# A sixth chunk with seven block products, w2's parts written over the weight sums, later key-value sums

## The chip, the cores and the metric

The kernel runs on one core of a Trainium2 chip. The core has TensorE (matrix products, with a separate weight load), VectorE, ScalarE and GpSimd, which work at the same time and wait for each other on semaphores, and SyncE, whose queue issues most of the loads and stores. In the profile they are PE (with PEld for the weight loads), DVE, ACT, POOL and SP. The metric is the time of one execution in microseconds; the times given are medians of several executions.

## The reference

One input x (2048 x 512) goes through two branches, and a gate mixes them.

```python
g = sigmoid((x * gate_w).sum(-1, keepdims=True))
# branch A: linear attention, 32 heads of 16 columns
q, k, v = heads(x @ wqkv)
phi(y) = concat([softmax(y @ w_phi), softmax(-(y @ w_phi))])
kv = sum over s of phi(k)[s]^T v[s];  z = sum over s of phi(k)[s]
a = (phi(q) kv / (phi(q) z + 1e-6)) @ wo
# branch B: 512 -> 1376 -> 512
b = mish(x @ w1 + b1) @ w2
out = g * a + (1 - g) * b
```

## The kernel before

**Two stages.** Stage A goes through the 2048 rows of x in eight chunks of 256, numbered 0 to 7 here as in the code, each of two tiles of 128 rows (t = 0, 1). It makes k, v and q of each tile. q is stored to memory (pqd); k gives the features E (differences from the largest and the smallest of each head, an exponential, sums, reciprocals, a scaling). From E and v come the key-value sums kvp, which stay in one PSUM buffer over all chunks, and E is added up into z. Stage B goes through four blocks of 512 rows: up product, Mish, down product, and for branch A the products with kv and wo.

**Split products.** Every operand is split into a high part (a rounded copy, made by ScalarE) and a low part (the remainder, made by VectorE or GpSimd). A product a w is high x high, high x low and low x high. One product of a tile (k0, k1, v0, v1, q0 or q1) is thus 12 matmuls with 512 columns.

**Chunks in FAST.** With x and the weights cut in two by rows and columns, four of the products (k and q of both tiles) can be made of seven block products (after Strassen and Winograd) of 6 matmuls each: 42 matmuls instead of 48. The seven products are s1 to s7. They need sums of blocks of x (`sa`, four additions on GpSimd; split into parts by `sh0`, `sh1` on ScalarE and `sl0`, `sl1` on GpSimd) and sums of blocks of the weights, made once: t1, t3, t2, t4, split by `h0` to `h3` and `l0` to `l3`. `bc` and `m7` are copies on ScalarE, `ca` and `qa` additions on VectorE. t1 to t3 lie in the tiles th and tl, which use the buffers w2a; t4 and the parts of the sums of x lie in sh and sl, which use the buffers w2b.

**Weights for stage B.** w1 and w2 are loaded in twelve pieces during stage A: `L0` to `L11` are loads (SyncE), `H` the high part (ScalarE), `O` the low part (GpSimd). Pieces 0 to 2 are w1a, 3 to 5 w1b, 6 to 8 w2a, 9 to 11 w2b; 5 and 11 have 512 columns, the others 1,024. The loads share two buffers, so a load waits for the `O` of the piece two before it. Pieces 6 to 11 write new tiles in the buffers w2a and w2b, and so wait until th, tl, sh and sl are no longer used.

**z.** The features of each chunk but the last two are added to two arrays in memory (zd) by an adding store from GpSimd's queue (`z0`, `z1`). In chunk 6 `zld` loads the first to the chip (zacc), `za` adds the second with an adding load through GpSimd's queue, and from there on `z0` and `z1` are additions on GpSimd.

**What sets the order.** Each engine runs its instructions in the order in which the code issues them. Strings of step names write that order out: FIRST for chunk 0, SECOND for 1, BEFORE for 2, SEVEN for each chunk in FAST, then THIRD, NEXT and LAST, and BLOCK strings for stage B. A name without a mark is a step of this chunk, ' of the chunk before, + of the block or part after, # a step on weights. Further steps: `xh`, `xl` split x of the next chunk, `ldx` loads x two chunks on, `mx mn d0 d1 E S rS ml` with the tile's number make the features, `ve` and `qe` copy v and q out of PSUM, `st` stores q, `kv` or `kk` makes the key-value sums (`kk` is the name where both chunks of a pair are taken in one place). `k`, `q` and some v products share three PSUM buffers in turn, so a product waits until the third last has been read out.

```python
FAST = range(3, 5)
at(key, f"ml{t}", lambda d=d: scale_by(d, V))
odd = c + 1 - c % 2
if odd + 1 in FAST:
    at(("A", odd + 1), "kk", kv)
else:
    at(key, "kv", kv)
```

Of the kernel before, what the change touches and what calls it, by code (L numbers as in the profile page):

```python
# [10 lines left out]
F32R = mybir.dt.float32r  # L11
# [4 lines left out]
P = 128  # L16
# [7 lines left out]
NCH = S // SC  # L24
# [7 lines left out]
GROW = FA % P  # L32
ORDER = [NFA - 1] + list(range(NFA - 1)) + list(range(NFA, NF))
WARM = 6
FAST = range(3, 5)

# [5 lines left out]
    S0 rS0 ml0 S1 rS1 ml1 q0 qe0 st0 q1 qe1 st1  # L42
"""
SECOND = """
    h0# h1# l0# h3# l1# l3# z0' z1' k0 xh mx0 mn0 d00 d10 xl ldx k1 E0 L0# L1# mx1 mn1 d01 d11 v0 E1 S0 rS0 ve0 ml0 t2# h2# z0
    v1 S1 rS1 ml1 ve1 q0 qe0 st0 q1 qe1 st1 l2# kv' kv
"""
BEFORE = """
    k0 z1' xh xl sa mx0 mn0 d00 d10 ldx k1 E0 H0# O0# L2# mx1 mn1 d01 d11 v0 E1 sh0 sl0 S0 rS0 ve0 ml0 z0
    v1 H1# O1# L3# S1 rS1 ml1 ve1 q0 qe0 st0 q1 sh1 sl1 qe1 st1  # L50
"""
SEVEN = """
    s1 bc s7 m7 kk s2 xh xl sa z1' mx0 mn0 s6 ca d00 d10 E0 ldx v0 ve0 sh0 sl0 more S0 rS0 s4 mx1 mn1 s5 qa st1 d01 d11 E1 ml0 z0
    v1 S1 rS1 s3 ve1 qe0 st0 ml1 sh1 sl1
"""
THIRD = """
    k0 z1' xh xl mx0 mn0 d00 d10 ldx k1 H6# E0 O6# L8# mx1 mn1 d01 d11 v0 H7# E1 O7# L9# S0 rS0 ml0 ve0 v1 H8# O8# L10# z0
    S1 rS1 ml1 ve1 q0 qe0 st0 q1 z1 qe1 st1 kv' kv
"""
NEXT = """  # L60
# [38 lines left out]
def tile_gated_mix(ctx: ExitStack, tc: tile.TileContext, xT, wv, wkT, wqT, bd, w1a, w1b, b1, w2a, w2b, wo, out):  # L99
# [23 lines left out]
    def k2(name, tag, dt=F32):  # L123
        return T([P, 512], dt, tag, {"pq": 3, "io": 4, "hl": 8}[tag], name)
# [81 lines left out]
    def at(key, name, fn):  # L206
        steps.setdefault((key, name), []).append(fn)
# [84 lines left out]
        pin(eng.tensor_mul(hv(d["E"][:, :]), hv(d["E"][:, :]), d["S"][:, :, None].to_broadcast([P, 2 * H, DH])))  # L292

    wkr, wqr = [T([P, NFB * 512], F32, "w1b", 2, n)[:, : KT * 512].rearrange("p (k f) -> p k f", f=512) for n in ("wkr", "wqr")]
    TT = [T([P, NFA * 512], F32R, "w2a", 2, n)[:, :].rearrange("p (i k f) -> p i k f", i=3, k=2) for n in ("th", "tl")]
    TS = [T([P, NFB * 512], F32R, "w2b", 2, n) for n in ("sh", "sl")]
    T4 = [t[:, :1024].rearrange("p (k f) -> p k f", k=2) for t in TS]
    SX = [t[:, 1024:2048].rearrange("p (i k f) -> p i k f", i=4, k=2) for t in TS]
    SR = []

    def tops():

        k0, k1, q0, q1 = raw = [x[:, i : i + 2, :] for x in (wkr, wqr) for i in (0, 2)]
        t1, t4, t3, t2 = raw
        hl = [(*(x[:, i, :, :] for i in range(3)), y) for x, y in zip(TT, T4)]
        at("W", "t1", lambda: pin(G_.tensor_sub(t1, k0, q0)))
# [82 lines left out]
    def a_ops(c):  # L389
        key = ("A", c)  # L390
        P_ = psA[c] = {}
        for t in range(2):
            d = {}
            Es[c, t] = d

            def k_(t=t):
                P_["k", t] = proj(xs[c], t, wkh, wkl, "a")

            def v_(t=t):
                P_["v", t] = proj(xs[c], t, wvh, wvl, "dn" if c or t else "kv")  # L400
# [24 lines left out]
            at(key, f"ve{t}", ve)  # L425
            if t and c in FAST:
                at(key, "qa", qa)
            else:
                at(key, f"qe{t}", qe)
            at(key, f"st{t}", st)  # L430
            feat_ops(key, t, lambda t=t: P_["k", t][:, :], d, t == 1 and c in FAST)
            at(key, f"ml{t}", lambda d=d: scale_by(d, V))

            def zs(t=t, d=d):
                if c >= NCH - 2:
                    end = c == NCH - 1
                    for sl in (slice(0, 512), slice(512, 1024)) if end and t else (slice(0, 1024),):
                        ins = pin(G_.tensor_add(Z["acc"][:, sl], Z["acc"][:, sl], d["E"][:, sl]))
                        if end and not sl.start:
                            tc.add_manual_dep(ins.ins, last[t].ins.name, SYNC, reason="VectorE's own sums first")  # L440
                elif c:
                    pin(G_.dma_start(zd[t][:, :], d["E"], accum_op=ALU.add))
                else:
                    pin(G_.dma_start(zd[t][:, :], d["E"]))

            at(key, f"z{t}", zs)
        if c == NCH - 2:
            def zld():
                Z["acc"] = k4("zacc", "z")
                pin(Sy.dma_start(Z["acc"], zd[0][:, :]))  # L450

            at(key, "zld", zld)
            at(key, "za", lambda: pin(G_.dma_start(Z["acc"], zd[1][:, :], accum_op=ALU.add)))

        def kv():
            if not kvs:
                kvs.append(psum("kvp", "kv")[:, : NG * 64].rearrange("p (g f) -> p g f", g=NG))
            (kvp,) = kvs
            for t in range(2):
                E, v = Es[c, t]["E"], vs[c, t]  # L460
                Ev = E[:, :].rearrange("p (a r b x) -> p b r a x", a=2, r=2, b=8)
                for u in range(8):
                    for r in range(2):
                        o = (u % 2) * 64 + 32 * r
                        mm(kvp[o : o + 32, u // 2, :], v[:, u * 64 + 32 * r : u * 64 + 32 * r + 32], Ev[:, u, r, :, :],
                           start=(c == 0 and t == 0 and u < 2), stop=(c == NCH - 1 and t == 1), skip_group_check=True)

        odd = c + 1 - c % 2
        if odd + 1 in FAST:
            at(("A", odd + 1), "kk", kv)  # L470
        else:
            at(key, "kv", kv)
        if c in FAST:
            fast_ops(c, key, P_)
# [395 lines left out]
    run(SECOND, ("A", 1), ("A", 0))  # L870
    run(BEFORE, ("A", 2), ("A", 1))
    for c in FAST:
        w = {3: "H2# O2# L4# H3# O3# L5#", 4: "H4# O4# L6# H5# O5# L7#"}[c]
        run(SEVEN.replace("more", w), ("A", c), ("A", c - 1))
    for c, text in ((NCH - 3, THIRD), (NCH - 2, NEXT), (NCH - 1, LAST)):
        run(text, ("A", c), ("A", c - 1), ("B", 0))
    for b in range(NB):
        run((BLOCK0, BLOCK1, BLOCK, BLOCK)[b], ("B", b), ("B", b - 1), ("B", b + 1))
# [61 lines left out]
```

## Time and profile before

| | |
|---|---|
| median of 3 runs | 457.06 us (456.77 to 458.35) |
| the profiled execution | 457.48 us |
| its span, first to last instruction | 455.6 us |
| TensorE's matmuls | 444.9 us busy, 2760 of them |
| VectorE | 318.3 us busy |
| ScalarE | 207.1 us busy |
| GpSimd | 153.7 us busy |
| mean granted clock of TensorE | 0.996 |

The page gives busy times by engine, a strip of forty slices, the queues, the chain of waits back from the last instruction, and groups of instructions. A row of a timeline has the start and the length in us, the engine, the line of the code, the operation, its tiles and shapes and a count; in square brackets stands how long the engine had been idle and what ended that. A row of TensorE's with x4 is four matmuls; since they overlap, the distance between two rows, not the length, is the pace. A row of waits has the total, the number and the longest. The row of a window has the stretch, its length, busy time and count of PE, PEld, DVE, ACT and POOL, the granted clock, the DMA share and GB/s. Rows of loads and stores give the count, KB and the median time from issue to landing.

### The profile page before, as it was taken

What the parts mean: (1) busy time and instruction counts of PE and PEld (TensorE: products, weight loads), DVE (VectorE), ACT (ScalarE), POOL (GpSimd) and SP (SyncE); (2) the same over time, 40 slices, a digit from 0 to 9 for tenths busy, and PEclk for the clock granted to TensorE, in tenths of its full rate; (3) what the DMA queues carried; (4) which work ended last, traced back from release to release, by engine and by line L of the source; (5) the groups of instructions that cost most, each with busy time, mean ns of one, the idle gap of its engine ahead of it and who ended that gap; (6) DMA issues with size and microseconds to landing.
All of it is one profiled execution on the core that took longest, in us unless ns stands there. A gap on an engine that the chain in (4) does not pass through costs nothing.

```text
span 455.6 us, 7013 instructions
## 1 busy us (share of the span) xinstructions
PE 444.9 (98%) x2760; PEld 363.6 (80%) x2760; DVE 318.3 (70%) x421; ACT 207.1 (45%) x286; POOL 153.7 (34%) x110
## 2 busy tenths in 40 slices
PE   7999699999999999999999999999999999999996
PEld 7888588888888888878787887887887888787885
DVE  2498887889597999979997985666967629611002
ACT  4772443726435564636347354434254553234220
POOL 2299465845724356320213212023212122221211
PEclk9999899999999999999999999999999999999999
DMA  7413845689596300222435050431141402030002
GB/s 281 160 62 122 201 125 139 149 204 264 163 322 149 116 24 1 72 68 71 138 101 154 17 148 21 109 114 54 24 117 56 112 19 92 1 81 13 1 0 94
DMA packets 27609, 47.41 MB, mean 104 GB/s; under 512 B 5940, under 2 KB 14132, under 8 KB 27576
## 3 DMA queue, kind: packets, MB, share of 16 engines
q1 hardware_dynamic: 25528, 39.88, 28.5%
q0 software_dynamic: 1904, 6.82, 7.8%
q8 instruction: 22, 0.36, 0.3%
q10 hardware_dynamic: 144, 0.26, 0.2%
q14 instruction: 11, 0.09, 0.1%
HBM read 23.87 MB, written 14.69 MB: 85 GB/s over the span
## 4 chain that ended last, share of the span: by engine, by line
PE 87%; DVE 0%; ACT 0%; issue 0%
PE up L111 27%; PE down L111 26%; PE proj L111 21%; PE wo L111 10%; PE num L111 2%; PE kvp L111 2%; DVE io L784 0%; ACT qs L131 0%; PE z L111 0%; ACT xh L131 0%; PE kvT L603 0%
## 5 line engine op out<-in xcount | busy, mean ns | idle before, releaser
L649 POOL TENSOR_TENSOR l<-act,h 128x512 fp32r<-128x512 f32 x44 | 61.4, 1397 | 219.1 <-ACT h L131 183.4
L131 ACT ACTIVATE act<-up,b1s 128x512 f32<-128x512 f32 x44 | 30.3, 688 | 88.6 <-PE up L111 88.5
L131 ACT ACTIVATE E<-E 128x1024 f32<-128x1024 f32 x32 | 33.6, 1060 | 55.6 <-DVE E L275 37.7
L292 DVE TENSOR_TENSOR E<-E,Sm 128x1024 f32<-128x1024 f32 x32 | 46.6, 1457 | 1.0
L281 DVE TENSOR_REDUCE Sm<-E 128x64 f32<-128x1024 f32 x32 | 38.7, 1211 | 4.9 <-ACT E L131 4.9
L111 PE MATMUL wo<-woh,ohl 128*128 128x512 f32 x128 | 40.8, 389 | 0.0
L111 PE MATMUL down<-w2ah,h 128*128 128x512 f32 x96 | 37.5, 390 | 0.0
L111 PE MATMUL down<-w2ah,l 128*128 128x512 f32 x96 | 37.4, 389 | 0.0
L111 PE MATMUL down<-w2al,h 128*128 128x512 f32 x96 | 37.3, 389 | 0.0
L784 DVE SCALAR_TENSOR_TENSOR io<-down,og_sb,io 128x512 f32<-128x512 f32 x16 | 11.1, 749 | 31.0 <-PE down L111 31.0
L111 PE MATMUL down<-w2bh,h 128*128 128x512 f32 x80 | 31.2, 390 | 0.0
L111 PE MATMUL down<-w2bl,h 128*128 128x512 f32 x80 | 31.1, 389 | 0.0
L111 PE MATMUL down<-w2bh,l 128*128 128x512 f32 x80 | 31.1, 389 | 0.0
L131 ACT ACT_TABLE_LOAD x20 | 25.7, 1283 | 10.4 <-PE up L111 10.1
L758 DVE TENSOR_TENSOR ohl<-num,ohl 128x512 fp32r<-128x512 f32 x16 | 10.2, 679 | 26.4 <-ACT ohl L131 26.4
L131 ACT ACTIVATE h<-act 128x512 fp32r<-128x512 f32 x44 | 27.8, 632 | 1.4
L111 PEld LDWEIGHTS wo<-woh,ohl 128*128 128x128 f32 x128 | 24.0, 188 | 5.1
L111 PE MATMUL up<-xbh,w1ah 128*128 128x512 f32 x96 | 26.2, 394 | 0.0
L111 PE MATMUL up<-xbh,w1al 128*128 128x512 f32 x96 | 25.7, 389 | 0.0
L111 PE MATMUL up<-xbl,w1ah 128*128 128x512 f32 x96 | 25.7, 389 | 0.0
L111 PE MATMUL wo<-wol,ohl 128*128 128x512 f32 x64 | 24.9, 389 | 0.0
L546 DVE TENSOR_TENSOR xbl<-xraw,xbh 128x1024 fp32r<-128x1024 f32 x8 | 10.0, 1288 | 19.8 <-ACT xbh L131 19.8
(156 smaller groups left out, 1006.0 us busy)
## 6 DMA issues: line engine op xcount, KB each, us to landing
xraw<-in_xT_dram SPq DMA_DIRECT2D x16, 512.0 KB, 5.4
eT<-tt SPq DMA_DIRECT2D x128, 64.0 KB, 2.0
zd<-E POOLq DMA_DIRECT2D x12, 512.0 KB, 6.6
pqd<-qs SPq DMA_DIRECT2D x16, 256.0 KB, 3.3
pq<-pqd SPq DMA_DIRECT2D x16, 256.0 KB, 2.9
out_dram<-io SPq DMA_DIRECT2D x16, 256.0 KB, 2.1
raw<-in_w1a_dram SPq DMA_DIRECT2D x3, 512.0 KB, 4.6
raw<-in_w2a_dram SPq DMA_DIRECT2D x3, 512.0 KB, 4.5
```

The costliest lines, as they stand in the source:

```text
L111: return pin(nc.tensor.matmul(*a, **k))
L131: return pin(A_.activation(out_, in_, fn, **k))
L281: pin(V.tensor_reduce(d["S"], hv(d["E"][:, :]), axis=AX.X, op=ALU.add))
L292: pin(eng.tensor_mul(hv(d["E"][:, :]), hv(d["E"][:, :]), d["S"][:, :, None].to_broadcast([P, 2 * H, DH])))
L546: last[h] = pin(V.tensor_sub(xb[b][1][:, :, sl], kt(raw[h], SC), f32(xb[b][0][:, :, sl])))
L649: pin(G_.tensor_sub(U[i]["l"], U[i]["a"], f32(U[i]["h"])))
L758: pin(V.tensor_sub(ohl[h, gp][:, 512:], num[h, gp], f32(ohl[h, gp][:, :512])))
L784: pin(V.scalar_tensor_tensor(io[t], dn[t], og_sb[:, i : i + 1], io[t], op0=ALU.mult, op1=ALU.add))
```

## The change

FAST takes chunk 5 in. Chunk 5 now runs by SEVEN; THIRD is gone. Pieces 6 to 11 of the weights are written into the tiles that hold the weight sums, part by part, so that a piece waits only for the readers of the columns that it overwrites. The additions of z on chip begin in chunk 5 instead of 6. The key-value sums of chunks 0 and 1 move into chunk 2, behind its k0, and those of 4 and 5 into chunk 6, behind its k0. h3, l1 and l3, h2 and l2 move from chunk 1 to chunk 2 or later in it, and two raw copies of the prologue come one weight split later. The pieces are now taken in the order 0 to 5, 11, 7, 8, 9, 6, 10.

```diff
-FAST = range(3, 5)
+FAST = range(3, 6)
...
 SECOND = """
-    h0# h1# l0# h3# l1# l3# z0' z1' k0 xh mx0 mn0 d00 d10 xl ldx k1 E0 L0# L1# mx1 mn1 d01 d11 v0 E1 S0 rS0 ve0 ml0 t2# h2# z0
-    v1 S1 rS1 ml1 ve1 q0 qe0 st0 q1 qe1 st1 l2# kv' kv
+    h0# h1# l0# z0' z1' k0 mx0 mn0 d00 d10 ldx k1 E0 L0# L1# xh mx1 mn1 d01 d11 v0 E1 S0 rS0 ve0 ml0 xl z0
+    v1 S1 rS1 ml1 ve1 q0 qe0 st0 q1 qe1 st1 t2#
...
+    s1 bc s7 m7 kk s2 xh xl zld sa z1' mx0 mn0 s6 ca d00 d10 E0 ldx v0 ve0 sh0 sl0 za more S0 rS0 s4 mx1 mn1 s5 qa st1 d01 d11 E1 ml0 z0
...
-    TT = [T([P, NFA * 512], F32R, "w2a", 2, n)[:, :].rearrange("p (i k f) -> p i k f", i=3, k=2) for n in ("th", "tl")]
-    TS = [T([P, NFB * 512], F32R, "w2b", 2, n) for n in ("sh", "sl")]
+    w2at = [T([P, NFA * 512], F32R, "w2a", 2, "w2a" + x) for x in "hl"]
+    TS = w2bt = [T([P, NFB * 512], F32R, "w2b", 2, "w2b" + x) for x in "hl"]
+    TT = [t[:, :].rearrange("p (i k f) -> p i k f", i=3, k=2) for t in w2at]
...
-                if c >= NCH - 2:
+                if c >= FAST[-1]:
...
-        if c == NCH - 2:
+        if c == FAST[-1]:
             def zld():
...
-        if odd + 1 in FAST:
+        if c <= FAST[-1]:
             at(("A", odd + 1), "kk", kv)
...
+    W["w2a"], W["w2b"] = (w2at, NFA * 512), (w2bt, NFB * 512)
...
-        w = {3: "H2# O2# L4# H3# O3# L5#", 4: "H4# O4# L6# H5# O5# L7#"}[c]
+        w = {3: "H2# O2# L4# H3# O3# L5#", 4: "H4# O4# L11# H5# O5# L7# H11# O11# L8#", 5: "H7# O7# L9# H8# O8# L6#"}[c]
         run(SEVEN.replace("more", w), ("A", c), ("A", c - 1))
-    for c, text in ((NCH - 3, THIRD), (NCH - 2, NEXT), (NCH - 1, LAST)):
+    for c, text in ((NCH - 2, NEXT), (NCH - 1, LAST)):
```

TensorE at the seam of chunks 1 and 2, before (E and v are features and values; the last two numbers of a row are the shape):

```order
L111 MATMUL proj_81_503<-wqh_15_122,xl_44_305 128x512 x2
L111 MATMUL kvp_83_520<-E_40_297,v_46_312 32x64 x16
L111 MATMUL kvp_83_520<-E_49_319,v_51_339 32x64 x16
L111 MATMUL kvp_83_520<-E_65_413,v_75_462 32x64 x16
L111 MATMUL kvp_83_520<-E_72_442,v_78_485 32x64 x16
L111 MATMUL proj_84_585<-wkh_11_118,xh_59_403 128x512 x2
```

and after:

```order
L107 MATMUL proj_81_498<-wqh_15_122,xl_44_305 128x512 x2
L107 MATMUL proj_87_524<-wkh_11_118,xh_66_427 128x512 x2
L107 MATMUL proj_87_524<-wkh_11_118,xh_67_428 128x512 x2
L107 MATMUL proj_87_524<-wkl_12_119,xh_66_427 128x512 x2
L107 MATMUL proj_87_524<-wkl_12_119,xh_67_428 128x512 x2
L107 MATMUL proj_87_524<-wkh_11_118,xl_68_429 128x512 x2
L107 MATMUL proj_87_524<-wkh_11_118,xl_69_430 128x512 x2
L107 MATMUL kvp_88_537<-E_40_297,v_46_312 32x64 x16
L107 MATMUL kvp_88_537<-E_49_319,v_51_339 32x64 x16
L107 MATMUL kvp_88_537<-E_61_404,v_75_457 32x64 x16
L107 MATMUL kvp_88_537<-E_72_437,v_78_480 32x64 x16
L107 MATMUL proj_92_612<-wkh_11_118,xh_66_427 128x512 x2
```

The twelve matmuls of chunk 2's k0 now stand ahead of the key-value sums.

ScalarE in chunk 4, from its first exponential to the copy of q (before):

```order
L131 ACTIVATE E_152_978<-E_152_978 128x1024
L131 ACTIVATE v_155_997<-proj_154_984 128x512
L131 ACTIVATE w1bh_129_805<-raw_128_803 128x1024
L131 ACTIVATE w1bh_129_805<-raw_131_809 128x512
L131 ACTIVATE E_162_1029<-E_162_1029 128x1024
L131 ACTIVATE v_165_1057<-proj_163_1035 128x512
L131 ACTIVATE qs_166_1059<-proj_143_877 128x512
```

and after, to the copies bc and m7 of chunk 5 (w2bh<-sraw are sh0 and sh1, w2bh<-raw is H11):

```order
L127 ACTIVATE E_153_983<-E_153_983 128x1024
L127 ACTIVATE v_156_1002<-proj_155_989 128x512
L127 ACTIVATE w2bh_21_130<-sraw_149_965 128x512
L127 ACTIVATE w1bh_129_805<-raw_128_803 128x1024
L127 ACTIVATE w1bh_129_805<-raw_131_809 128x512
L127 ACTIVATE w2bh_21_130<-raw_157_1008 128x512
L127 ACTIVATE E_164_1040<-E_164_1040 128x1024
L127 ACTIVATE v_167_1068<-proj_165_1046 128x512
L127 ACTIVATE qs_168_1070<-proj_143_877 128x512
L127 ACTIVATE w2bh_21_130<-sraw_149_965 128x512
L127 ACTIVATE proj_171_1084<-proj_169_1076 128x512
L127 ACTIVATE m7_172_1092<-proj_170_1077 128x512
```

H11 now stands between the two exponentials of chunk 4.

GpSimd from the stores of z of chunk 4 on, before (zd and zacc are the sums of z, w2al and w2bl the low parts of w2):

```order
L442 DMA zd0_124<-E_152_978 128x1024
L442 DMA zd1_125<-E_162_1029 128x1024
L513 TENSOR_TENSOR w2al_178_1108<-raw_156_1001,w2ah_177_1107 128x1024
L513 TENSOR_TENSOR w2al_178_1108<-raw_157_1005,w2ah_177_1107 128x1024
L513 TENSOR_TENSOR w2al_178_1108<-raw_179_1112,w2ah_177_1107 128x1024
L442 DMA zd0_124<-E_174_1089 128x1024
L442 DMA zd1_125<-E_182_1118 128x1024
L513 TENSOR_TENSOR w2bl_208_1314<-raw_184_1137,w2bh_207_1313 128x1024
L513 TENSOR_TENSOR w2bl_208_1314<-raw_188_1160,w2bh_207_1313 128x1024
L453 DMA zacc_205_1298<-zd1_125 128x1024
```

and after:

```order
L511 TENSOR_TENSOR w2bl_22_131<-raw_157_1008,w2bh_21_130 128x512
L439 DMA zd0_124<-E_153_983 128x1024
L335 TENSOR_TENSOR w2bl_22_131<-sraw_149_965,w2bh_21_130 128x512
L439 DMA zd1_125<-E_164_1040 128x1024
L450 DMA zacc_177_1108<-zd1_125 128x1024
L511 TENSOR_TENSOR w2al_20_129<-raw_158_1012,w2ah_19_128 128x1024
L511 TENSOR_TENSOR w2al_20_129<-raw_159_1016,w2ah_19_128 128x1024
L435 TENSOR_TENSOR zacc_177_1108<-zacc_177_1108,E_181_1123 128x1024
L435 TENSOR_TENSOR zacc_177_1108<-zacc_177_1108,E_191_1175 128x1024
L511 TENSOR_TENSOR w2bl_22_131<-raw_185_1147,w2bh_21_130 128x1024
```

The adding load of zacc (za) now comes before the low parts of pieces 7 and 8, and the two adding stores of chunk 5 have become additions behind them.

More of the change, by code (lines that the diff above doesn't have):

```diff
@@ L44 @@
 SECOND = """
-    h0# h1# l0# h3# l1# l3# z0' z1' k0 xh mx0 mn0 d00 d10 xl ldx k1 E0 L0# L1# mx1 mn1 d01 d11 v0 E1 S0 rS0 ve0 ml0 t2# h2# z0
-    v1 S1 rS1 ml1 ve1 q0 qe0 st0 q1 qe1 st1 l2# kv' kv
+    h0# h1# l0# z0' z1' k0 mx0 mn0 d00 d10 ldx k1 E0 L0# L1# xh mx1 mn1 d01 d11 v0 E1 S0 rS0 ve0 ml0 xl z0
+    v1 S1 rS1 ml1 ve1 q0 qe0 st0 q1 qe1 st1 t2#
 """
 BEFORE = """
-    k0 z1' xh xl sa mx0 mn0 d00 d10 ldx k1 E0 H0# O0# L2# mx1 mn1 d01 d11 v0 E1 sh0 sl0 S0 rS0 ve0 ml0 z0
+    z1' xh xl k0 kk h3# l1# l3# mx0 mn0 d00 d10 k1 E0 sa ldx h2# mx1 mn1 d01 d11 v0 E1 H0# O0# L2# l2# S0 rS0 ve0 ml0 sh0 sl0 z0
     v1 H1# O1# L3# S1 rS1 ml1 ve1 q0 qe0 st0 q1 sh1 sl1 qe1 st1
@@ L52 @@
 SEVEN = """
-    s1 bc s7 m7 kk s2 xh xl sa z1' mx0 mn0 s6 ca d00 d10 E0 ldx v0 ve0 sh0 sl0 more S0 rS0 s4 mx1 mn1 s5 qa st1 d01 d11 E1 ml0 z0
+    s1 bc s7 m7 kk s2 xh xl zld sa z1' mx0 mn0 s6 ca d00 d10 E0 ldx v0 ve0 sh0 sl0 za more S0 rS0 s4 mx1 mn1 s5 qa st1 d01 d11 E1 ml0 z0
     v1 S1 rS1 s3 ve1 qe0 st0 ml1 sh1 sl1
 """
[L56 to L59, printed above, removed]
 NEXT = """
-    lq0+ k0 xh xl mx0 mn0 d00 d10 ldx zld k1 H9# E0 O9# ldw0 L11# mx1 mn1 d01 d11 H10# E1 O10# ldw1 za S0 rS0 ml0 z0 v0 ve0 H11# O11#
+    lq0+ z1' k0 kk xh xl mx0 mn0 d00 d10 ldx k1 H9# E0 O9# ldw0 L10# mx1 mn1 d01 d11 H6# E1 O6# ldw1 S0 rS0 ml0 z0 v0 ve0 H10# O10#
     S1 rS1 ml1 z1 v1 ve1 q0 mx0+ mn0+ d00+ d10+ qe0 st0 q1 qe1 st1 E0+ lq1+
@@ L832, in tile_gated_mix @@
     fsplit(wkh, wkl, 2)
-    raw_k(0)
-    raw_k(1)
     k_part(0)
@@ L837, in tile_gated_mix @@
     fsplit(wkh, wkl, 3)
+    raw_k(0)
+    raw_k(1)
     k_part(1)
```

## The prediction

> **What bounds the kernel now.** I read the page's busy times first, then the waits of TensorE, then the chain of waits for the pace of a full stretch.
>
> ```profile
> PE 444.9 (98%) x2760; PEld 363.6 (80%) x2760; DVE 318.3 (70%) x421; ACT 207.1 (45%) x286; POOL 153.7 (34%) x110
> ...
> PE kvp L111 <- ACT xh L131: 3.5, 1, 3.5
> ...
> 40.00:60.00 20.00, 15.98 (x182) 12.93 (x182) 17.02 (x19) 6.01 (x9) 11.50 (x11) 0.91 0.58 141
> ...
> 166.53 2.72 PE down L111 x12
> ```
>
> TensorE is busy for 98% of the span. After the start it waits in one place only, ahead of the key-value sums (kvp) of chunk one; in that stretch, 40 to 60 us, it is busy for 15.98 us of 20 and its granted clock is 0.91. Everywhere else 12 matmuls of 512 columns take 2.72 us, so one costs 2.72 / 12 = 0.227 us. The time can fall by that one wait and by matmuls taken out, and it rises by every new wait of TensorE. The timeline of TensorE has the wait, and the same kind of work without it:
>
> ```profile
> 46.40 1.07 PE L111 MATMUL proj<-wqh,xl 128*128 128x512 f32 x4
> ...
> 53.17 1.08 PE L111 MATMUL kvp<-E,v 128*32 128x64 f32 x32 [3.46 <-ACT xh L131]
> 54.18 2.08 PE L111 MATMUL proj<-wkh,xh 128*128 128x512 f32 x4
> ...
> 58.01 1.08 PE L111 MATMUL proj<-wkh,xh 128*128 128x512 f32 x4
> ...
> 88.84 0.61 PE L111 MATMUL proj<-th,sl 128*128 128x512 f32 x2
> 89.39 1.99 PE L111 MATMUL kvp<-E,v 128*32 128x64 f32 x128
> ...
> 91.89 0.62 PE L111 MATMUL proj<-wkl,xh 128*128 128x512 f32 x2
> ```
>
> From 46.40 to 58.01 us (11.61 us) stand 16 matmuls of 512 columns and 128 of the sums. From 88.84 to 91.89 (3.05 us) stand 4 and 128, without a wait. Twelve more at 0.227 make 5.77 us. The wait, with the slow group behind it (2.08 us where 1.07 is usual), costs 11.61 - 5.77 = 5.84 us.
>
> **The change part by part.**
>
> *Sums later (chunk one).* TensorE goes from chunk one's last q product straight to k0 of chunk two; the sums follow. Are their inputs ready? The timelines of ScalarE and VectorE in chunk one:
>
> ```profile
> 37.86 1.06 ACT L131 ACTIVATE sh<-wkr 128x1024 fp32r<-128x1024 f32 x1 [4.19 <-POOL wkr L309]
> 38.83 1.14 ACT L131 ACTIVATE xh<-xraw 128x512 fp32r<-128x512 f32 x2
> 39.87 1.04 ACT L131 ACTIVATE E<-E 128x1024 f32<-128x1024 f32 x1
> ...
> 39.48 4.06 DVE L258 TENSOR_TENSOR xl<-xraw,xh 128x512 fp32r<-128x512 f32 x2 [1.51 <-ACT xh L131]
> ...
> 51.80 1.23 DVE L292 TENSOR_TENSOR E<-E,Sm 128x1024 f32<-128x1024 f32 x1
> ```
>
> Without sh and xh ahead of it the first exponential starts at 38.0 instead of 39.87. VectorE no longer spends 4.06 us on xl beside three operations of GpSimd; it does the differences of the second half first (to 40.4), then S0, rS0, ml0, xl, S1, rS1, ml1. Adding 1.2, 0.6, 1.2, 1.2, 1.2, 0.6, 1.2 from 40.4 ends ml1 at about 47.6, where it ended at 53.0. TensorE reaches k0 at 47.3 and the sums of the last tile at 47.3 + 2.7 + 1.5 = 51.5, so 4 us of slack: I take the whole 5.84 us as gone. The bounds are 0 (the wait stays) and 5.84. The two raw copies moved in the prologue, and the loads' new order, I cost at nothing: ScalarE stood idle before its next use there, and the pieces arrive several us before they are used, except where a term below says otherwise.
>
> *Seven products in chunk five.* Four products of 12 matmuls become seven of 6: 6 fewer, 6 x 0.227 = 1.36 us. It adds four sums and two remainders on GpSimd, four copies on ScalarE and one add on VectorE; chunks three and four carry the same load without a wait of TensorE.
>
> *Weight sums l1 and l3 move into chunk two.* They go to GpSimd beside ml0 and ml1 of chunk two. The rows that price this, from the timelines of VectorE and GpSimd, and the starts of chunks three and four with the first add of chunk three:
>
> ```profile
> 68.10 2.71 POOL L513 TENSOR_TENSOR w1al<-raw,w1ah 128x1024 fp32r<-128x1024 f32 x1
> 70.46 1.60 POOL L338 TENSOR_TENSOR sl<-sraw,sh 128x512 fp32r<-128x512 f32 x1
> ...
> 112.32 2.42 POOL L513 TENSOR_TENSOR w2al<-raw,w2ah 128x1024 fp32r<-128x1024 f32 x1 [1.90 <-ACT w2ah L131]
> ...
> 29.75 2.47 DVE L292 TENSOR_TENSOR E<-E,Sm 128x1024 f32<-128x1024 f32 x1
> ...
> 68.15 5.01 DVE L292 TENSOR_TENSOR E<-E,Sm 128x1024 f32<-128x1024 f32 x1
> ...
> 78.14 0.69 DVE L376 TENSOR_TENSOR proj<-proj,m 128x512 f32<-128x512 f32 x1
> ...
> 71.62 0.62 PE L111 MATMUL proj<-wkh,xh 128*128 128x512 f32 x2
> ...
> 86.58 0.62 PE L111 MATMUL proj<-wkh,xh 128*128 128x512 f32 x2
> ```
>
> Now GpSimd's remainder sl1 ends at 72.1, 0.4 us into chunk three; ml1 ends 1.1 us later. After the change chunk three begins at 71.62 - 5.84 = 65.8. An operation of GpSimd of 1,024 columns takes 2.42 us, so by estimate it does l1 from 48.2, l3 to 53.4, the sums sa to 56.9, O0 from 59.5 (ScalarE's cast ahead of it) to 62.0, sl0 to 63.3; ml0, held as in the rows, ends at 64.5 and releases its store; O1 and sl1 end near 69.9. If ml1 is again held until then it ends at 71.0; xl, two reductions and the add (1.3 + 1.2 + 0.7) end at 74.2. The product s4, which needs the add, comes 36 matmuls after the chunk's start, at 65.8 + 8.2 = 74.0. So 0.3 us late, between 0 (ml1 held as in the 2.47 us row) and 2. The Trainium skill, SBUF — State Buffer, "Who interferes with whom", says that whichever of the two engines issues first holds the shared port for one whole instruction, and the other then goes. The 2.47 us row agrees; the 5.01 us row does not, since it outlasts two instructions of GpSimd. By that rule this term would be zero and the sum 0.3 us lower.
>
> *H11 ahead of chunk four's second exponential.* This is the one new place where ScalarE waits for a load: piece 11 is loaded only once O4 has freed its buffer, and ScalarE's next work (the exponential, v's and q's evictions, the copy bc that TensorE's s6 of chunk five needs) stands behind it. I keep the profile's times from here on, leaving out the shift so far. Timelines of ScalarE, SyncE's queue and TensorE, and the page's landing times:
>
> ```profile
> 80.05 1.06 ACT L131 ACTIVATE E<-E 128x1024 f32<-128x1024 f32 x1 [3.83 <-DVE E L275]
> ...
> 96.33 1.06 ACT L131 ACTIVATE E<-E 128x1024 f32<-128x1024 f32 x1 [5.20 <-issue]
> ...
> 102.19 1.06 ACT L131 ACTIVATE E<-E 128x1024 f32<-128x1024 f32 x1 [2.85 <-DVE E L273]
> ...
> 139.17 0.63 ACT L131 ACTIVATE w2bh<-raw 128x512 fp32r<-128x512 f32 x1 [7.18 <-DMA raw<-in_w2b_dram]
> ...
> 85.90 3.74 SPq L169 DMA_DIRECT2D raw<-in_w1b_dram  x2
> ...
> 130.36 0.51 SPq L169 DMA_DIRECT2D raw<-in_w2b_dram  x1
> ...
> 103.68 1.07 PE L111 MATMUL proj<-wkh,xh 128*128 128x512 f32 x4
> ...
> raw<-in_w1b_dram SPq DMA_DIRECT2D x1, 256.0 KB, 2.8
> ```
>
> Chunk three has the same order up to there: its load L4 is issued 85.90 - 80.05 = 5.85 us after the first exponential, so L11 at 96.33 + 5.85 = 102.2. A quarter megabyte landed in 2.8 us once, and in 139.17 - 130.36 = 8.8 us once (this same piece, in a crowded stretch). I take 2.8, since the earlier loads are then nearly in: H11 at 105.0, the exponential at 105.5 instead of 102.19, bc done 3.1 us later, at 108.6. TensorE wants it at 103.68 plus 18 matmuls, 107.8: 0.8 us. VectorE, whose S1 waits for the exponential, has that, a sum, a reciprocal, a scaling, xl, two reductions and the add of chunk five to go through, 1.1 + 1.2 + 0.6 + 1.2 + 1.3 + 1.2 + 0.7 = 7.3 us, to 112.8, when TensorE, so delayed, wants it: together 1.1 us, with 8.8 us landing 7.1.
>
> *Sums of z on chip from chunk five.* zld now waits in SyncE's queue for chunk four's store of z0, and GpSimd's za waits for zld; O7, O8, the adds, O9 and L10 are queued behind za, H10 behind L10, and q0's eviction in chunk six behind H10. TensorE's k1 of chunk seven takes q0's PSUM buffer.
>
> ```profile
> zd<-E POOLq DMA_DIRECT2D x12, 512.0 KB, 6.6
> ...
> raw<-in_w2b_dram SPq DMA_DIRECT2D x2, 512.0 KB, 4.4
> ...
> zacc<-zd SPq DMA_DIRECT2D x1, 512.0 KB, 6.4
> zacc<-zd POOLq DMA_DIRECT2D x1, 512.0 KB, 6.6
> ...
> DMA to landing us min/median/max: 3.0/6.5/11.0
> ...
> 143.12 2.39 POOL L438 TENSOR_TENSOR zacc<-zacc,E 128x1024 f32<-128x1024 f32 x1 [5.84 <-DMA zacc<-zd]
> ...
> 88.85 1.51 DVE L292 TENSOR_TENSOR E<-E,Sm 128x1024 f32<-128x1024 f32 x1
> ```
>
> (The row of minimum, median and maximum is that of the twelve stores zd.) z0's store goes out at 106.9, after O11; +6.5 is 113.4; +6.4 is 119.8 for za; O7 then runs to 123.1 and O8 to 125.5. The load za lands at 126.4, two adds end at 131.2, O9 at 133.6, L10 lands at 138.0, and H10 with two evictions ends at 140.1. TensorE ends chunk five at 103.68 + 66 x 0.227 + 1.1 = 119.7, and k1 of chunk seven comes at 119.7 + 2.7 + 2.1 + 16.3 = 140.8, plus the next term: about 1 us of slack, no cost. But ml1 of chunk five now lies beside O7: in chunk three ml1 began 88.85 - 86.58 = 2.27 us after the chunk's end, so here at 122.0, and TensorE wants it at 119.7 + 2.7 + 1.5 = 124.0. Held as in the 2.47 us row, which also began inside an operation of GpSimd, it ends at 124.5: 0.5 us; as in the 5.01 us row 2.6; free, 0. I take 0.5.
>
> *Sum.* The profiled execution took 457.48 us (span 455.60 and 1.88 around it). 457.48 - 5.84 - 1.36 + 0.3 + 1.1 + 0.5 = 452.18. The median of the runs shown, 457.06, is 0.42 below that execution: 451.8 us.
>
> **The rivals.**
> - All new waits are hidden (ml1 slips in, L11 lands before H11): 457.48 - 7.20 - 0.42 = 449.9. For it: TensorE ran for 400 us without a wait. Against: H11's load cannot leave before O4.
> - Piece 11 lands late, as in the 8.8 us row: 7.1 instead of 1.1 us, and the clock falls once more as after the 3.46 us wait (1.0): 458.8, within 0.5% of before.
> - GpSimd is held by za. With both z transfers through GpSimd's queue at the largest landing, 11.0, and L10 at 8.8, H10's chain ends at 140.1 + 4.5 + 4.4 + 4.4 = 153.4; k1 waits 153.4 - 141.3 = 12.1, and 1.0 for the clock: 451.8 + 13.1 = 464.9, slower. It decides against the change from some 8 us of added landing on. For it: these rows lie in the same crowded stretch. Against: medians leave the slack.
> - The wait of chunk one only moves: if ml1 still ended at 53.0, TensorE would idle 1.5 us behind k0, so 453.3 at most; it stays faster.
>
> **How the numbers follow.** What a measurement of this kernel tells from no change is 0.5%, 2.3 us: faster is below 454.8, slower above 459.3. My own sum has 0.46 (450.7 to 454.5), all hidden 0.23, late piece 0.12 (half-late ones still faster), za 0.11, the moved wait 0.08. Faster: 0.46 + 0.23 + 0.08 = 0.77; same 0.12; slower 0.11. The range runs from 449.6, just under the case with all hidden, to 457.5, into the late piece; it leaves out za and the worst of the late piece.
>
> **What would show it.** Right: TensorE without a gap from 47 to 52 us and no group of 2.08 us; 2754 matmuls; small waits of TensorE on ScalarE near 102 us and on VectorE near 117 and 68. Wrong: a wait of TensorE above 3 us at chunk five's s6, at the sums in chunk six, or at k1 of chunk seven, with ScalarE waiting for a raw piece or GpSimd for zacc.

## The result, and the profile after

The changed kernel takes 460.3 us (median of 5 executions, 458.63 to 460.79), where the kernel before takes 457.06. The ratio is 1.0059, with a 95% interval of 1.004 to 1.0079. So it is slower by about 0.6%, and the prediction, 451.8 us and faster (449.6 to 457.5), was wrong in its sign and in its range. The profiled execution took 458.63 us, with a span of 456.7.

Chunks are counted from 0 here, as before. Some of the quoted expectations count them from 1; the text behind each names the place again.

The page of the changed kernel, busy times and the chain that ended last:

```profile
PE 443.1 (97%) x2754; PEld 361.0 (79%) x2754; DVE 332.9 (73%) x423; ACT 208.5 (46%) x289; POOL 164.2 (36%) x116
...
PE 65%; DVE 7%; issue 1%
```

and TensorE's waits after it (total, number, longest):

```profile
PE kvp L107 <- DVE E L288: 4.1, 1, 4.1
PE proj L107 <- ACT proj L127: 1.8, 1, 1.8
...
PE proj L107 <- DVE proj L373: 1.0, 1, 1.0
```

TensorE has its 2754 matmuls, six fewer, but VectorE is now 7% of the chain, and there is a wait of 4.1 us for VectorE that the kernel before did not have and the prediction did not name. TensorE's timeline after shows both ends of the story:

```profile
46.07 1.07 PE L107 MATMUL proj<-wkh,xh 128*128 128x512 f32 x4
...
48.88 1.99 PE L107 MATMUL kvp<-E,v 128*32 128x64 f32 x128
50.80 1.20 PE L107 MATMUL proj<-wkh,xh 128*128 128x512 f32 x4
...
103.08 0.73 PE L107 MATMUL proj<-wkh,xh 128*128 128x512 f32 x2 [1.78 <-ACT proj L127]
...
139.52 1.10 PE L107 MATMUL kvp<-E,v 128*32 128x64 f32 x64
...
156.36 1.08 PE L107 MATMUL kvp<-E,v 128*32 128x64 f32 x32 [4.05 <-DVE E L288]
157.37 2.08 PE L107 MATMUL up<-xbh,w1ah 128*128 128x512 f32 x4
```

The seam of chunks 1 and 2 has no gap any more (46.07 to 50.80). TensorE reaches the first sums of chunk 7 at 139.52, then waits 4.05 us for the last tile's scaled features, and stage B begins at 157.37. The same two rows before:

```profile
144.00 1.10 PE L111 MATMUL kvp<-E,v 128*32 128x64 f32 x64
...
157.16 1.20 PE L111 MATMUL up<-xbh,w1ah 128*128 128x512 f32 x4
```

TensorE had come 4.5 us earlier to chunk 7's sums, and all of it was given back within the rest of that chunk. The two windows of 20 us (length, then busy time and count of PE, PEld, DVE, ACT, POOL, then clock) say who was busy there, before:

```profile
120.00:140.00 20.00, 20.00 (x208) 16.75 (x208) 14.51 (x20) 6.97 (x10) 8.49 (x6) 1.00 0.93 250
```

and after:

```profile
120.00:140.00 20.00, 20.00 (x142) 16.33 (x134) 19.86 (x20) 7.14 (x9) 18.70 (x8) 1.00 0.69 230
```

VectorE has the same 20 instructions, in 19.86 instead of 14.51 us; GpSimd is busy for 18.70 us instead of 8.49. Both engines' timelines after, VectorE first:

```profile
118.02 1.51 DVE L288 TENSOR_TENSOR E<-E,Sm 128x1024 f32<-128x1024 f32 x1
119.45 5.69 DVE L254 TENSOR_TENSOR xl<-xraw,xh 128x512 fp32r<-128x512 f32 x2
...
137.95 1.69 DVE L269 TENSOR_TENSOR E<-pq,mx 128x512 f32<-128x512 f32 x1
139.56 2.89 DVE L271 TENSOR_TENSOR E<-mn,pq 128x512 f32<-128x512 f32 x1
...
154.36 1.85 DVE L288 TENSOR_TENSOR E<-E,Sm 128x1024 f32<-128x1024 f32 x1
```

```profile
115.10 0.88 POOL L450 DMA_DIRECT2D zacc<-zd  x1 [8.93 <-DMA zacc<-zd]
115.67 6.10 POOL L511 TENSOR_TENSOR w2al<-raw,w2ah 128x1024 fp32r<-128x1024 f32 x2
121.73 5.66 POOL L435 TENSOR_TENSOR zacc<-zacc,E 128x1024 f32<-128x1024 f32 x2
...
135.71 3.38 POOL L511 TENSOR_TENSOR w2bl<-raw,w2bh 128x1024 fp32r<-128x1024 f32 x1
139.06 2.85 POOL L435 TENSOR_TENSOR zacc<-zacc,E 128x1024 f32<-128x1024 f32 x1
```

GpSimd waits 8.93 us before it can issue za. Behind za stand O7, O8 and the two additions of z, and they come out without a pause, 115.67 to 127.4 us, with O9 and O6 right after them. Right there VectorE has to split x for chunk 7 (xl), and the pair takes 5.69 us. A second heap comes after a pause of 1.23 us, an addition, O10 and another addition, and meets the differences of q (pq), 1.69 and 2.89 us. The kernel before, VectorE:

```profile
121.35 1.29 DVE L258 TENSOR_TENSOR xl<-xraw,xh 128x512 fp32r<-128x512 f32 x2 [2.55 <-ACT xh L131]
125.07 0.69 DVE L266 TENSOR_REDUCE mx<-proj 128x32 f32<-128x512 f32 x1 [2.42 <-PE proj L111]
...
137.38 0.68 DVE L273 TENSOR_TENSOR E<-pq,mx 128x512 f32<-128x512 f32 x1
137.98 0.69 DVE L275 TENSOR_TENSOR E<-mn,pq 128x512 f32<-128x512 f32 x1
141.39 0.69 DVE L266 TENSOR_REDUCE mx<-proj 128x32 f32<-128x512 f32 x1 [2.72 <-PE proj L111]
...
154.37 1.91 DVE L292 TENSOR_TENSOR E<-E,Sm 128x1024 f32<-128x1024 f32 x1
```

The account of VectorE, from the start of xl to the end of the last scaling: before, 121.35 to 156.28 is 34.9 us, of which it waited 2.42 + 2.72 and three times 0.2 us, so its work takes about 29.1. After, 119.45 to 156.21 is 36.8 without a wait. That is 7.7 us more, nearly all in two places: 5.69 - 1.29 = 4.4 for xl and 1.69 + 2.89 - 1.37 = 3.2 for the differences. TensorE was ready for the result at 156.36 - 4.05 = 152.3. Undisturbed, and if it never had to wait for TensorE, VectorE would have been done at 119.45 + 29.1 = 148.6, 3.7 us ahead; 7.7 - 3.7 = 4.0 is the wait. (This is an account of one trace and comes out by construction; whether GpSimd's order is the cause, e1 and e6 test.)

### The profile page after: what moved, and what is told of

Read it like the earlier page. It is cut to its first block, busy times and chain, and to the rows that moved or that the text cites. A ratio compares the mean times of both kernels' runs of the same rounds, so it can differ in the third digit from the quotient of the medians.

```text
span 456.7 us, 7015 instructions
## 1 busy us (share of the span) xinstructions
PE 443.1 (97%) x2754; PEld 361.0 (79%) x2754; DVE 332.9 (73%) x423; ACT 208.5 (46%) x289; POOL 164.2 (36%) x116
## 4 chain that ended last, share of the span: by engine, by line
PE 65%; DVE 7%; issue 1%
PE up L107 27%; PE down L107 26%; PE wo L107 10%; PE num L107 2%; DVE E L288 1%; DVE E L271 1%; DVE Sm L277 1%; DVE E L269 1%; DVE mx L262 1%; DVE xl L254 1%; DVE Sm L285 0%; DVE io L782 0%; DVE mn L262 0%; PE kvp L107 0%; PE z L107 0%
## 5 line engine op out<-in xcount | busy, mean ns | idle before, releaser
L647 POOL TENSOR_TENSOR l<-act,h 128x512 fp32r<-128x512 f32 x44 | 60.2, 1370 | 220.5 <-ACT h L127 184.8
L288 DVE TENSOR_TENSOR E<-E,Sm 128x1024 f32<-128x1024 f32 x32 | 49.1, 1534 | 1.0
```

The costliest lines, as they stand in the source:

```text
L647: pin(G_.tensor_sub(U[i]["l"], U[i]["a"], f32(U[i]["h"])))
```

## The experiments

Theory P (the port): the work of GpSimd that piles up behind za comes out as one burst beside VectorE's two-operand work, and VectorE becomes what ends stage A. Rival L (piece 11): ScalarE's wait for the load of piece 11 is the main loss. Rival W (amount): GpSimd simply has too much to do with the sixth chunk run by SEVEN, wherever that work stands. The first expectations also name a load theory: VectorE itself has too much to do from chunk 5 on, whoever works beside it. The table has all runs. "Sums" is the time at which the key-value sums at the seam begin and "B" the time at which stage B begins, both in the profiled execution. From B to the end of the span it is 298.4 us, or up to 2 more where a long wait left TensorE's clock low, so what differs lies ahead of B.

| kernel | median us | ratio to before, interval | sums | B | between |
|---|---|---|---|---|---|
| changed | 460.3 | 1.0059 (1.004 to 1.0079) | 48.88 | 157.37 | 108.5 |
| e1_za_behind | 455.92 | 0.9982 (0.9949 to 1.0016) | 48.00 | 153.69 | 105.7 |
| e2_h11_behind | 459.66 | 1.008 (1.0034 to 1.0126) | 48.09 | 154.59 | 106.5 |
| e3_seam_alone | 452.86 | 0.9916 (0.9884 to 0.9948) | 48.30 | 151.27 | 103.0 |
| e4_six_alone | 465.39 | 1.0177 (1.013 to 1.0224) | - | 163.05 | - |
| e5_both_behind | 453.6 | 0.9927 (0.9894 to 0.9959) | 48.58 | 152.83 | 104.3 |
| e6_z_late | 459.18 | 1.0027 (0.9999 to 1.0055) | 49.07 | 154.84 | 105.8 |
| e7_seam_sums | 450.42 | 0.985 (0.9821 to 0.9878) | 50.19 | 151.40 | 101.2 |
| e8_z_late_h11 | 454.93 | 0.9947 (0.9927 to 0.9967) | 49.13 | 153.49 | 104.4 |
| e9_all_three | 452.4 | 0.9896 (0.9876 to 0.9917) | 48.55 | 152.00 | 103.5 |
| e7_again | 450.97 | 0.987 (0.9847 to 0.9893) | 49.31 | 150.52 | 101.2 |
| e3_again | 453.59 | 0.9944 (0.9911 to 0.9976) | 49.40 | 152.63 | 103.2 |
| after_again | 462.96 | 1.0133 (1.0065 to 1.0201) | 49.32 | 164.44 | 115.1 |

The kernel before had medians of 457.16, 457.71 and 457.36 us in the three groups of runs (first four, next four, last four of the table's experiments).

### e1: za behind the low parts

```diff
- ... ve0 sh0 sl0 za more S0 rS0 s4 ...
+ ... ve0 sh0 sl0 more za S0 rS0 s4 ...
```

> Changed kernel, with the adding load za behind O7 and O8 in GpSimd's queue instead of ahead of them. Port theory (GpSimd's work piles up behind za and comes out in one burst beside VectorE's xl of chunk seven, which takes 5.69 us instead of 1.29, and stage A ends with VectorE): xl takes 1.3 to 2.5 us, TensorE's wait of 4.05 us at chunk seven's sums falls below 1.5 and the slow group behind it goes: 455 to 456.5 us. Load theory (VectorE has too much to do from chunk five on, whoever is beside it): 460, the wait stays at 4 us. Piece-11 theory (ScalarE's wait for piece 11 makes VectorE late): 460, since that wait is not touched.

Measured: 455.92 us. VectorE's groups from 115 to 158 us:

```profile
L271 DVE TENSOR_TENSOR E<-mn,pq 128x512 f32<-128x512 f32 x2 | 3.6, 1784 | 0.0
L269 DVE TENSOR_TENSOR E<-pq,mx 128x512 f32<-128x512 f32 x2 | 2.4, 1188 | 0.0
L254 DVE TENSOR_TENSOR xl<-xraw,xh 128x512 fp32r<-128x512 f32 x2 | 1.3, 684 | 0.0
```

No instruction was taken out; one load went two places back in GpSimd's queue. xl is 1.3 us again, of TensorE's waits in stage A only those of 1.8 and 1.0 are left, and the median is 4.4 us lower. The differences of q are as long as before the edit, and without xl's 4.4 us VectorE just keeps ahead (7.7 - 4.4 = 3.3 is less than the 3.7 us). Both engines have the same instructions as in the changed kernel, so neither the load theory nor W can explain the 4.4 us. Theory P holds, in place and in size. From the seam's sums to B it is only 2.8 us less than in the changed kernel, although chunk 7 has lost its whole wait. In this execution TensorE ran slowly behind the wait of 1.8 us for piece 11 (granted clock 0.65 from 104 to 108 us). From the end of that wait to the sums of chunks 4 and 5 it needed 16.78 us, 1.6 more than in the changed kernel.

### e2: piece 11 behind the sums of x for chunk 5 (sh1, sl1)

```diff
- 4: "H4# O4# L11# H5# O5# L7# H11# O11# L8#"
+ 4: "H4# O4# L11# H5# O5# L7#"       and " H11# O11# L8#" at the end of chunk 4
```

> Changed kernel, with H11, O11 and L8 behind sh1 and sl1 of chunk four instead of ahead of its second exponential. Piece-11 theory: VectorE's wait of 3.06 us and TensorE's of 1.78 us go, and with them most of the loss: 455 us or less, wait at chunk seven's sums below 2 us. Port theory: the two waits go, but za and the burst behind it come earlier by the same 3 us, so xl still takes over 4 us and TensorE still waits some 3 to 4 us at chunk seven's sums: 457 to 459. Load theory: as the port theory, 457 to 458.

Measured: 459.66 us. The wait of 1.8 us on ScalarE is gone, but:

```profile
PE kvp L107 <- DVE E L288: 4.1, 1, 4.1
```

```profile
L254 DVE TENSOR_TENSOR xl<-xraw,xh 128x512 fp32r<-128x512 f32 x2 | 5.7, 2876 | 0.0
```

Stage B begins 2.8 us earlier than in the changed kernel, 0.8 of it because the seam does. The burst came along with its chunk and cost the same: the wait behind it is 4.06 us. Rival L is a second, smaller loss and not the main one. The median hardly moved (460.3 to 459.66) and lies just above the 457 to 459 that P expected; the executions spread widely, and the profiled one, 456.63 us, is the shortest.

### e3 and e4: each half alone

e3 is the kernel before with the new orders of chunks 1 and 2; e4 is the changed kernel with the old ones.

```diff
  e3, from the kernel before:
- SECOND, BEFORE, the two raw copies as before;   if odd + 1 in FAST:
+ SECOND, BEFORE, the two raw copies as changed;  if c < 2 or odd + 1 in FAST:
  e4, from the changed kernel:
- SECOND, BEFORE, the two raw copies as changed;  if c <= FAST[-1]:
+ SECOND, BEFORE, the two raw copies as before;   if 2 <= c <= FAST[-1]:
```

> Kernel before, with the order of chunks one and two and the prologue of the changed kernel alone (sums of chunks zero and one behind k0 of chunk two); chunk five, the pieces and the sums of z as before. Port theory: VectorE waited for TensorE before (2.4 and 2.7 us in chunks six and seven), so it can follow; the 5.84 us come through but for a wait for the piece loads: 451.5 to 454. Load theory: the end of stage A is VectorE's and does not move: 456 to 458, with a wait of TensorE of 4 us and more at chunk seven's sums. The wait at the seam itself is gone by both.

> Changed kernel with the order of chunks one and two and the prologue as before (the wait of TensorE at the seam of chunks one and two comes back, 5.84 us). Port and piece-11 theories: TensorE is late by 5.84 us, so VectorE's lateness in chunks six and seven falls into that: the wait at chunk seven's sums goes, 459 to 461.5, about the time of the changed kernel. If each part instead has its price by itself: 460.3 + 5.8 = 466.

Measured: 452.86 and 465.39 us, 4.3 less and 8.2 more than before. In e3 only one wait is left behind the start, 0.9 us at s4 of chunk 3. e4 has all the others:

```profile
PE kvp L107 <- DVE E L288: 4.6, 2, 4.1
PE kvp L107 <- ACT xh L127: 3.5, 1, 3.5
```

My expectation for e4 fell. I had thought that the 4.1 us wait exists only because TensorE arrives 4.5 us early, so that the old wait at the seam would swallow it. It does not: 8.2 - 4.3 = 3.9, near the 3.2 us that the whole change costs. za waits for transfers that start with chunk 4's store of z, so the burst has its place in the chunks, not in time: za goes out 11.85 us after TensorE's wait for piece 11 has ended, where it was 12.02 in the changed kernel. The wait at the end is there whether chunk 5 begins early or late. The two halves simply add.

### e5: both moved

e1's and e2's edits together.

> The load of the z sums stands behind the two low parts of chunk six on GpSimd's queue, and piece 11 of w2 stands behind the sums of chunk five, both together. If the port was the main loss and the wait for piece 11 a separate second one, the two add: 455.9 with the load behind, less the 1.8 us that the sums of chunk six still wait for the copy there, gives 453.5 to 454.8, and no wait of 1.8 us on ScalarE is left in the trace. If the two long differences of chunk eight (3.6 and 2.4 us in both runs so far) still keep VectorE as what ends stage A, taking the 1.8 us away gives nothing: 455.5 to 456.5.

Measured: 453.6 us, and no wait of 1.8 us on ScalarE. The two losses are separate and add. But two smaller waits have come up that the changed kernel hid behind the larger ones; TensorE's timeline:

```profile
118.93 0.65 PE L107 MATMUL kvp<-E,v 128*32 128x64 f32 x32 [0.98 <-DVE E L288]
...
136.68 1.21 PE L107 MATMUL proj<-wkh,xh 128*128 128x512 f32 x4 [0.55 <-ACT qs L127]
```

The first is the sums of chunks 4 and 5, late because ml0 of chunk 5 lies beside O8 (2.67 us instead of 1.2). The second is k1 of chunk 7, which waits for q's eviction behind H10.

### e6 and e8: z as before, without and with e2's edit

```diff
- SEVEN: xl zld sa ... sl0 za more ...      NEXT: ldx k1 ... ldw1 S0
+ SEVEN: xl sa ... sl0 more ...             NEXT: ldx zld k1 ... ldw1 za S0
- if c >= FAST[-1]:  (z added on chip)      if c == FAST[-1]:  (zld, za)
+ if c >= NCH - 2:                          if c == NCH - 2:
```

> The changed kernel, with the sums of z as in the kernel before: chunk six still adds by DMA, and the two loads of the z sums stand in chunk seven. GpSimd is then spared the two additions of chunk six (2.4 to 2.9 us each) and isn't held before the low parts 7 and 8. If the burst behind the held load is the cause, xl of chunk seven is 1.3 us again, the wait for the scaled sums there goes, and the time is 454.5 to 457, as with the load moved behind. If it is the amount of GpSimd's work in the sixth chunk with its seven products, the time stays at 459 to 460.5. If the load now holds the low parts of chunk seven instead and the burst comes one chunk later, beside the differences of chunk eight, it is 457 to 460 with the wait at chunk eight.

> The sums of z as before, and piece 11 behind the sums of chunk five, together. By the sum of the parts it is 1.0 to 1.8 us less than with the sums of z as before alone, and so 453 to 455.5 by the burst theory; if GpSimd's amount of work is the cause it is 457.5 to 459.

Measured: 459.18 and 454.93 us. In e6's profile xl and the differences are as short as in the kernel before:

```profile
L271 DVE TENSOR_TENSOR E<-mn,pq 128x512 f32<-128x512 f32 x2 | 1.4, 683 | 0.0
L269 DVE TENSOR_TENSOR E<-pq,mx 128x512 f32<-128x512 f32 x2 | 1.4, 680 | 0.0
L254 DVE TENSOR_TENSOR xl<-xraw,xh 128x512 fp32r<-128x512 f32 x2 | 1.3, 685 | 0.0
```

Of the wait at chunk 7's sums 0.58 us is left. The trace of e6 is what P expects (455.04 us in the profiled execution), its median what W expects. That execution is the fastest of ten; the others reach to 460.6, with granted clocks down to 0.991. e8, with the same work for GpSimd and without the wait of 1.9 us on piece 11, lies at 454.93 in P's range, which speaks against W. That e6's median is 4.3 us above e8's where 1.0 to 1.8 were expected is not settled: the wait for piece 11 and the clock behind it would do it, as e1's trace shows, but no trace of one of e6's longer executions was taken.

### e7 and e9: the weight sums left in chunk 1

```diff
- SECOND: h0# h1# l0# z0' z1' k0 ...               BEFORE: ... k0 kk h3# l1# l3# mx0 ...
+ SECOND: h0# h1# l0# h3# l1# l3# z0' z1' k0 ...   BEFORE: ... k0 kk mx0 ...
```

e7 is e3 with this edit, e9 is e5 with it.

> The orders of chunks two and three alone (452.9), with the three steps of the weight sums (the copy of one, two low parts on GpSimd) left in chunk two as before. In the orders alone they stand in chunk three, where GpSimd holds the port against xl (6.1 us for 1.3) and the product s4 waits 0.9 us for VectorE. If that is what the wait comes from, xl is 1.3 us, the wait goes, and the time is 451.5 to 452.3. If the low parts hold VectorE in chunk two instead, the wait moves there: 452.6 to 454.

> The changed kernel with three places mended at once: the load of the z sums behind the low parts 7 and 8, piece 11 behind the sums of chunk five, and the steps of the weight sums left in chunk two. With the first two the profile began stage B at 152.83 us; the 1.0 us wait of the fourth sum of chunk four should go as it did with the orders alone, so stage B begins near 151.9 and the time is 451.5 to 453.5. Against the orders with the weight sums in chunk two (stage B at 151.40) the seven products of chunk six are then worth nothing: their six fewer products (1.36 us) are spent on the 1.0 us wait at kv of chunks five and six and the 0.55 us wait for a buffer in chunk seven, which both stay. Rival: the two waits go with the fourth sum's, since all of chunk four to six comes 1 us earlier, and the seven products show: stage B at 150.0 to 150.6, time 449 to 450.5.

Measured: 450.42 us for e7, below what I expected, and 452.4 for e9. In e7 TensorE waits for nothing behind the first products. e7 was run once more, with e3 and e9 on the same chip:

> The orders of chunks two and three with the weight sums left in chunk two, once more, beside the orders alone on the same chip: the two profiles began stage B at 151.40 and 151.27 us and so promise the same time, while the medians of different calls lay 2.4 us apart (450.4 and 452.9). By the profiles both are 451 to 452.9 and within 1 us of each other; by the medians this one is 449.5 to 451.5 and the other 452 to 454.

> The orders of chunks two and three alone, once more: 451 to 452.9 and within 1 us of the version with the weight sums in chunk two by the profiles, 452 to 454 by the medians.

Measured: 450.97 and 453.59 us, so the medians were right and the likeness of the two first profiles was not. The table says why. From the seam's sums to stage B it is 101.2 us in both profiles of e7, 103.0 and 103.2 in those of e3. But the sums began at 50.19 in the first profile of e7 and at 48.30 in that of e3: the start, which waits for loads, differs by 1.1 us between the two profiles of e3 and by 0.9 between those of e7, and the 1.9 us between the two first profiles had hidden the difference. VectorE shows where the 2 us come from, in e7_again and in e3_again:

```profile
50.27 1.29 DVE L258 TENSOR_TENSOR xl<-xraw,xh 128x512 fp32r<-128x512 f32 x2
...
71.49 0.69 DVE L376 TENSOR_TENSOR proj<-proj,m 128x512 f32<-128x512 f32 x1
```

```profile
47.99 6.10 DVE L258 TENSOR_TENSOR xl<-xraw,xh 128x512 fp32r<-128x512 f32 x2
...
73.59 0.68 DVE L376 TENSOR_TENSOR proj<-proj,m 128x512 f32<-128x512 f32 x1
```

With l1 and l3 beside it xl takes 6.10 us, and the addition that s4 needs comes 2.1 us later.

e9 against e7_again prices all that the change does beyond the seam, with the mended orders on both sides: the seven products of chunk 5 together with z on chip, the new places of w2's pieces and the later sums of chunks 4 and 5. It is 1.4 us more, where the seven products alone were to give 1.36 less; no run has the seven products without the rest. e9 has waits of 1.0 us at the sums of chunks 4 and 5 and of 1.6 at k1 of chunk 7. The latter in TensorE's and ScalarE's timelines:

```profile
135.89 1.20 PE L107 MATMUL proj<-wkh,xh 128*128 128x512 f32 x4 [1.61 <-ACT qs L127]
```

```profile
133.81 1.06 ACT L127 ACTIVATE w2bh<-raw 128x1024 fp32r<-128x1024 f32 x1 [8.98 <-DMA raw<-in_w2b_dram]
...
135.25 1.08 ACT L127 ACTIVATE qs<-proj 128x512 f32<-128x512 f32 x2
```

H10 waits 8.98 us for piece 10, and the evictions stand behind it. e7 is the fastest version of all and beats both kernels, with ratios of 0.985 and 0.987 in two groups of runs.

### The changed kernel once more

> The changed kernel itself, beside its mended version on the same chip: 458.5 to 461.5, and 6 to 9 us above the version with three places mended.

Measured: 462.96 us, 10.6 above e9, both more than I expected. This time the profile caught another collision. VectorE and TensorE:

```profile
119.59 6.12 DVE L288 TENSOR_TENSOR E<-E,Sm 128x1024 f32<-128x1024 f32 x1
...
129.16 3.45 DVE L254 TENSOR_TENSOR xl<-xraw,xh 128x512 fp32r<-128x512 f32 x2
```

```profile
129.38 0.87 PE L107 MATMUL kvp<-E,v 128*32 128x64 f32 x32 [2.87 <-DVE E L288]
```

za went out at 118.97, 11.3 us after TensorE's wait for piece 11 had ended, instead of 12.0, so the burst met ml0 (6.12 us) first and xl (3.45) only with its rest, and TensorE waited in chunk 6 already (and for 2.40 us in chunk 4, where a scaling of 3.51 us had met another low part). In both profiles some operation of VectorE's pays for the burst; which one differs with when za goes out.

## Why the prediction was wrong

- *Sums later, -5.84.* Right. The wait and the slow group are gone. e7, the orders without their one side effect, is 6.4 and 7.3 us below before in two groups of runs. That is 0.6 to 1.5 more than the term, and no run says where the rest comes from.
- *Seven products, -1.36.* The matmuls fell by six, but e9 against e7, which has all the rest of the change too, shows none of it in the time. The sentence "chunks three and four carry the same load without a wait of TensorE" was the weak one: chunk 5 has that load and, in the same stretch, z on chip and three pieces of w2.
- *l1 and l3 in chunk two, +0.3.* Right place and mechanism, undersized: 0.97 us of wait in the changed kernel, and about 2 us in all by e3 against e7. I had let l1 and l3 hold ml0 and ml1, but not xl, which stands beside them and took 6.11 us in the changed kernel and 6.10 in e3_again.
- *H11, +1.1.* Right mechanism, undersized: 1.78 us, and at s2 instead of s6, six matmuls (1.36 us) earlier than the sum had it. The load took 2.6 us, nearly what I assumed (2.8). In e1 the slow groups behind this wait cost 1.6 us more, which the sum left out. e2 takes the wait out.
- *ml1 of chunk five beside O7, +0.5.* The sums of chunks 4 and 5 waited 0 in the first profile, 0.98 in e5, and 0.28 + 2.87 in the second profile of the changed kernel, above the upper bound of 2.6. It is ml0 that was held, not ml1, and how long is different in each execution.
- *"no cost" of the sums of z.* This is the step that failed. I listed the right queue, "O7, O8, the adds, O9 and L10 are queued behind za, H10 behind L10, and q0's eviction in chunk six behind H10", followed it to ScalarE, PSUM and k1 of chunk 7, found 1 us of slack and stopped. I did not ask what the queue does when it is released. GpSimd then works without a pause for 16 us (115.67 to 132.1), and VectorE, whose two-operand work stands beside it, pays 4.4 us there and 3.2 more at the second heap. TensorE's wait of 4.05 us comes from the two together: e1 takes the first away, e6 both, and the wait falls to 0 and 0.58 us. I had the row for the price (5.01 us for one scaling) and used it for chunk 2 and for one term of chunk 5 only. And the prediction says nothing of VectorE's waits on TensorE in chunks 6 and 7, 2.42 and 2.72 us; they were the slack that a faster TensorE uses up.
- *The rivals.* "GpSimd is held by za" named the cause and missed the mechanism: it asked for some 8 us of late landings, while zld landed 6.0 us after its issue (109.10 to 115.10), less than the 6.4 I had assumed, and that was enough. k1 of chunk 7 did become a wait, of 0.55 and 1.61 us, but only in e5 and e9, where TensorE comes earlier. "The wait of chunk one only moves" was excluded by e3.
- *The sum.* With the waits of the profile, 157.16 - 5.84 - 1.36 + 0.97 + 1.78 + 4.05 = 156.8, against 157.37 measured for the start of stage B; the 0.6 us between them is not explained, and the start alone differs by more than that between executions. The slow first group of stage B adds about 1 behind that mark.

## What to carry to other kernels

When an instruction that waits for a transfer moves up a queue, price the release too: list what is queued behind it, add up how long that runs without a pause, and see what the neighbour on the same port has to do in that time. An engine's waits for the bottleneck engine are slack that the speed-up itself spends, so compare its bare work (29.1 us here) with the stretch it will have, before calling it idle. And compare profiles between two marks inside the program, since the start alone moved by up to 1.1 us between two profiles of one kernel here.

## What the runs showed of the hardware

A VectorE instruction can be held through two of GpSimd's in a row: the scaling at 119.59 lasts 6.12 us, through O7 and O8 (119.53 to 124.6) and its own 1.1. The Trainium skill, SBUF — State Buffer, "Who interferes with whom", says that a VectorE instruction with two SBUF inputs contends with a GpSimd instruction that reads SBUF; all the long rows here are of that kind, while the reductions beside the burst stay at 0.68 us, and so do the differences of k (126.26 us), of whose two inputs one lies in PSUM, which agrees. It gives the pair of ports to whoever issues first for one whole instruction; for this row, which outlasts two, that is too short.

Waits below 2 us can cost TensorE its clock, or not. In the second profile of the changed kernel, a wait of 1.88 us that ended at 107.66 was followed 1.5 us later by slow groups; behind one of 1.80 us at the same place in e1 stood slow groups too. The waits of 1.78 us in the first profile and of 1.89 us in e6, again at the same place, were not. TensorE and then the window of the second profile:

```profile
107.66 0.73 PE L107 MATMUL proj<-wkh,xh 128*128 128x512 f32 x2 [1.88 <-ACT proj L127]
...
109.15 1.01 PE L107 MATMUL proj<-w2ah,w2bh 128*128 128x512 f32 x2
```

```profile
104.00:112.00 8.00, 6.12 (x21) 4.64 (x20) 6.27 (x8) 5.10 (x9) 4.25 (x4) 0.82 0.88 199
```

The Trainium skill, TensorE: Matmul & The Clock Gate, "What's actually happening", puts the half-rate clock behind an idle window of about 3.4 us that runs freely. That the length of the wait alone does not decide agrees with a free-running window; that 1.80 us was enough does not agree with a whole idle window. Whether such waits also make the times of a kernel scatter was not tested: e1 and e6 spread over 6.0 and 5.6 us and e7, which waits nowhere behind the first products, over 2.3 and 0.6, but e3, whose one wait there is about 1 us, spread over 5.5 and 5.6.
